# A fused attention and channel-mix kernel with its PSUM banks, its instruction order and its engine choices written anew

## The chip, the cores and the metric

The kernel runs on one core of one Trainium2 chip. The metric is the device time of one execution in microseconds (us). The time before is 250.7 us, the median of three runs (250.73, 250.70, 248.66).

A core has five engines that run their own instruction lists in order and wait for each other by semaphores: PE (matmuls; its weight loads are shown apart as PEld), DVE, ACT and POOL for work on tiles, and SP, which here only issues DMAs. PE writes PSUM alone, which has eight banks of 512 float32 columns; DVE and ACT read PSUM, POOL does not.

## The reference

Inputs are q, k, v of 4 batches, 8 heads, 768 positions, 64 channels, a projection of 64 x 6, and the weights of a channel mix. What is computed:

```python
q_bits = einsum(q, proj) > 0                    # 6 bits a row, the same for k
mask = q_bucket[..., None] == k_bucket[..., None, :]
scores = where(mask, q @ k.T / 8, -1e9)
attn = exp(scores - max); attn /= attn.sum(-1) + 1e-9
x = (attn @ v)                                  # heads side by side: B, 768, 512
xk = mu_k * x + (1 - mu_k) * x_prev             # x_prev: one position earlier
xr = mu_r * x + (1 - mu_r) * x_prev
kk = relu(xk @ w_k) ** 2                        # 512 -> 1024
out = sigmoid(xr @ w_r) * (kk @ w_v)            # 1024 -> 512
```

## The kernel before, in words

**Pairs.** The 32 heads are worked in 16 pairs of two heads (n = 0 to 15, four pairs a batch). For a pair the kernel loads q and k (lines 471 to 481) and v (486), scales q and k into a float16 upper part (`hi`, lines 556, or 554 on ACT) and subtracts it for a lower part (`lo`, 559), and lets a DMA transpose (`tr`, 563) put both into tile `a`, with channels on the partitions. Pairs 0 and 1 are prepared by head instead (`add_prep_first`: 616 to 621), transposed on PE (635) and copied out of PSUM (639).

**Bits.** `bits` (587) multiplies `a` with the projection, 24 matmuls in column groups. DVE turns the signs into numbers (`bx`, 591), and two or four small DMAs from SP (`row`, 599) put them as six extra rows into `a`, so that a score of rows whose bits differ falls far below the others and its exponential vanishes. For pair 0 the bits go straight into `a` (657, then 663 on ACT or 665 on DVE).

**Scores and values.** A pair has nine score steps of 1024 columns, two PSUM banks each: two to four matmuls (708), then one exponential on ACT (712) into `pt`. The value product (`oo`, 736 and 741) takes 36 matmuls of 65 columns in three slices; DVE divides by the row sum (`rc`, `ob`, 751 to 758). The result is transposed (DMA 768, or PE 794 and a copy 798), shifted by one position (`xs`, 776 and 778) and mixed (829 to 841) into `xk` and `xr`. The sums over v that a row without a partner needs (`vsum`, 509 to 515) and a bfloat16 copy of v (`va`, 501) run on POOL or DVE.

**MLP.** After four pairs a batch's MLP can start: `kp` (859, four matmuls of 384 columns, 64 such groups in all), ReLU on ACT (864) or DVE (866), a square on DVE (869), `r` (884) and its tanh (887), `v` (896), the product (903) and the store (907).

**What sets the order.** Each operation is put into a plan with `add(engine, duration, ...)`. `add_on` gives a choice of engines, taken from the table `WHERE` (line 40). The list `ORDER` (line 70) is the written sequence of all 1386 operations; each engine's instructions follow it. `schedule` (line 199 on) walks it and, with the durations of the plan, gives each score step the pair of banks among (0,1), (2,3), (4,5) and each other PSUM tile the bank among 7 to 3 that comes free first. The two mu vectors of 512 values are loaded by ACT's queue value by value (422) and lowered by one on DVE (424). Seven matmuls on zeros run at the start (390). The SP queue issues loads, transposes, rows and stores in one order.

The choice of engines for `hi` (line 568) is an example of `add_on`, with duration, whether it takes the SBUF access that DVE and POOL share in the plan, and the call:

```python
add_on({"DVE": (DVE_C(768 * m, 2), 1, lambda hi=hi: hi(nc.vector)), "ACT": (ACT_C(768 * m), 0, lambda hi=hi: hi(nc.scalar)),
        "POOL": (2.15 * m, 1, lambda hi=hi: hi(nc.gpsimd))}, R("hi", n), f"hi{n}", f"hi{n}{side}", r=rn, w=nh_h)
```

In the lists below an operation is named as in the code: `sc7_6` is score step 6 of pair 7, `hi4q` the upper part of q of pair 4, `kp0_1_1` half 1 of the second 128 columns of batch 0's first MLP product. Head 0 of a pair has j = 0, the second head j = 1.

Of the kernel before, what the change touches and what calls it, by code (L numbers as in the profile page):

```python
# [16 lines left out]

LAG = {"PE": 0.21, "ACT": 0.21, "DVE": 0.15, "POOL": 0.18, "SP": 1.8, "GQ": 2.0}
# [17 lines left out]
def R(kind, n):  # L36
# [99 lines left out]
class Plan:  # L136
# [42 lines left out]
    def sequence(self):  # L179
        if ORDER:  # L180
            return [self.ops[i] for i in ORDER]
# [17 lines left out]
    def schedule(self):  # L199
# [9 lines left out]
        for o in order:  # L209
            e = "POOL" if o.eng == "GQ" else o.eng  # L210
            if o.svc and o.eng != "GQ":
                queue.append(o)
# [752 lines left out]
```

## Time and profile before

| | |
|---|---|
| median of three runs | 250.7 us |
| the runs | 250.73, 250.70, 248.66 us |
| span of the profiled execution | 251.3 us |
| first exponential starts | 13.81 us |
| last matmul ends | 248.1 us |
| PE, DVE, ACT, POOL busy | 236.9, 195.4, 179.1, 27.9 us |
| instructions of PE, DVE, ACT, POOL | 2609, 471, 225, 73 |
| exponentials (line 712) | 144, mean 1.040 us, together 138.8 us |
| DMA | 44.56 MB, mean 177 GB/s |

A row of a timeline gives start, duration, engine, line, operation, tiles (out<-in) and shape, and in brackets the idle time of the engine before it and what ended it. `SPq` and `ACTq` are DMA issues of these queues. Rows of groups give count, busy time, mean duration in ns, idle time before and what ended most of it. Matmuls overlap, so one matmul's duration is longer than its share of PE's time; the time from start to start counts. Idle time of an engine that nobody waits for costs nothing.

### The profile page before, as it was taken

How to read it: one execution, taken by the hardware profiler on the slowest of the kernel's cores; microseconds unless marked ns; L12 is line 12 of the kernel's file. 1: busy time of each engine (PE TensorE's matmuls, PEld its weight loads, DVE VectorE, ACT ScalarE, POOL GpSimd, SP SyncE). 2: the span in 40 equal slices, each digit the busy share in tenths (PEclk: the TensorE clock that was granted, in tenths of full speed). 3: DMA queues.
4: the chain of work that ended last, by engine and by line, in shares of the span. 5: the costliest groups of instructions: out<-in, count | busy, mean ns of one | idle time of the engine just before them, and what ended most of it. 6: DMA issues, size and time to landing. Idle time of an engine off the chain costs nothing.

```text
span 251.3 us, 6510 instructions
## 1 busy us (share of the span) xinstructions
PE 236.9 (94%) x2609; PEld 147.6 (59%) x2609; DVE 195.4 (78%) x471; ACT 179.1 (71%) x225; POOL 27.9 (11%) x73
## 2 busy tenths in 40 slices
PE   6886799999799998999999999999999999999993
PEld 2444578876566655666467566655865654545442
DVE  3795679889788889898998999899787878376322
ACT  5596689999799978996878899988787223332220
POOL 5002240541302031100001100100000000000000
PEclk9799799999999999999999999999999999999998
DMA  6999999999989999999999996793231030022223
GB/s 187 308 178 251 220 215 191 267 249 189 213 292 241 204 293 292 273 201 269 184 333 186 184 185 158 210 230 57 90 64 44 0 128 28 13 83 86 83 85 125
DMA packets 75194, 44.56 MB, mean 177 GB/s; under 512 B 55524, under 2 KB 70172, under 8 KB 75164
## 3 DMA queue, kind: packets, MB, share of 16 engines
q1 hardware_dynamic: 74028, 44.15, 72.8%
q8 instruction: 20, 0.33, 0.6%
q10 hardware_dynamic: 1136, 0.01, 0.3%
q14 instruction: 10, 0.08, 0.1%
HBM read 24.12 MB, written 6.29 MB: 121 GB/s over the span
## 4 chain that ended last, share of the span: by engine, by line
PE 75%; DMA 11%; DVE 8%; SPq 3%; ACT 1%; issue 1%; DVEq 0%
PE ps_all L708 19%; PE ps_all L896 17%; PE ps_all L859 13%; PE ps_all L741 12%; PE ps_all L884 8%; DMA nat<-in_k_dram 5%; PE ps_all L587 4%; DMA nat<-in_q_dram 3%; DMA a<-bx 2%; DMA os<-in_moe_w_k_dram 1%; DVE nh L559 1%; DVE nh L556 1%; PE ps_all L736 1%; ACT pt L712 1%; PE ps_all L794 1%
## 5 line engine op out<-in xcount | busy, mean ns | idle before, releaser
L712 ACT ACTIVATE pt<-ps_all 128x1024 bf16<-128x1024 f32 x144 | 138.8, 1040 | 21.1 <-PE ps_all L708 19.8
L708 PE MATMUL ps_all<-a 128*128 128x512 f16 (+3 forms) x408 | 80.6, 318 | 5.1 <-DMA a<-bx 3.9
L708 PEld LDWEIGHTS <-a 128*128 128x128 f16 x408 | 35.3, 98 | 26.7 <-DMA a<-bx 4.7
L859 PE MATMUL ps_all<-xk,wk 128*128 128x384 bf16 x256 | 49.0, 326 | 0.9 <-DVE kr L866 0.9
L896 PE MATMUL ps_all<-wv,k 128*128 128x512 bf16 (+1 forms) x200 | 45.9, 370 | 0.6 <-DVE os L903 0.6
L741 PEld LDWEIGHTS <-pt 128*128 128x128 bf16 x1152 | 42.1, 98 | 6.9 <-issue 1.1
L741 PE MATMUL ps_all<-va,pt 128*128 128x65 bf16 x1152 | 43.9, 194 | 0.0
L859 PEld LDWEIGHTS <-wk 128*128 128x128 bf16 x256 | 24.5, 98 | 17.6 <-issue 1.6
L896 PEld LDWEIGHTS <-k 128*128 128x128 bf16 x200 | 19.4, 98 | 20.6 <-issue 0.7
L864 ACT ACTIVATE kr<-ps_all 128x384 bf16<-128x384 f32 x33 | 15.8, 493 | 19.2 <-DVE k L869 12.7
L887 ACT ACTIVATE rs<-ps_all 128x512 f32<-128x512 f32 x24 | 14.2, 603 | 20.9 <-PE ps_all L884 19.0
L559 DVE SCALAR_TENSOR_TENSOR nh<-nat,nh 128x768 f16<-128x768 f32 x28 | 27.3, 976 | 1.1 <-ACT nh L554 0.6
L903 DVE SCALAR_TENSOR_TENSOR os<-rs,ps_all 128x512 f32<-128x512 f32 (+1 forms) x25 | 16.5, 662 | 14.7 <-PE ps_all L896 9.9
L869 DVE TENSOR_TENSOR k<-kr 128x384 bf16<-128x384 bf16 x64 | 21.5, 350 | 3.7 <-ACT kr L864 3.5
L884 PE MATMUL ps_all<-wr,xr 128*128 128x512 bf16 x96 | 23.8, 379 | 0.0
L866 DVE TENSOR_SCALAR kr<-ps_all 128x384 bf16<-128x384 f32 x31 | 17.1, 555 | 8.3 <-PE ps_all L859 6.6
L758 DVE TENSOR_TENSOR ob<-ps_all,rc 128x384 bf16<-128x384 f32 (+1 forms) x36 | 18.3, 511 | 1.0
L884 PEld LDWEIGHTS <-xr 128*128 128x128 bf16 x96 | 9.0, 98 | 10.0 <-ACT kr L864 0.3
L587 PE MATMUL ps_all<-a,p0g 128*32 128x256 f16 (+1 forms) x180 | 13.4, 276 | 1.3 <-DMA a<-nh 1.3
L556 DVE TENSOR_SCALAR nh<-nat 128x768 f16<-128x768 f32 x22 | 12.3, 557 | 3.0 <-DMA nat<-in_q_dram 2.5
L587 PE MATMUL ps_all<-a,p1g 128*32 128x256 f16 (+1 forms) x180 | 12.9, 273 | 0.0
L841 DVE TENSOR_TENSOR xr<-tm,xt 128x768 bf16<-128x768 f16 (+1 forms) x18 | 9.4, 520 | 0.4
(94 smaller groups left out, 187.4 us busy)
## 6 DMA issues: line engine op xcount, KB each, us to landing
vn<-in_v_dram SPq DMA_DIRECT2D x16, 384.0 KB
out_dram<-os SPq DMA_DIRECT2D x23, 256.0 KB
nat<-in_k_dram SPq DMA_DIRECT2D x15, 384.0 KB
nat<-in_q_dram SPq DMA_DIRECT2D x15, 384.0 KB
wst<-in_moe_w_k_dram SPq DMA_DIRECT2D x2, 512.0 KB
wst<-in_moe_w_r_dram SPq DMA_DIRECT2D x2, 512.0 KB
wst<-in_moe_w_v_dram SPq DMA_DIRECT2D x2, 512.0 KB
a<-bx SPq DMA_DIRECT2D x48, 9.0 KB
```

Source lines behind the costliest of these rows:

```text
L559: nc.vector.scalar_tensor_tensor(out=nh[:, :, D:P], in0=nat.rearrange("p j (c d) -> p (j c) d", d=D), scalar=QS, in1=nh[:, :, 0:D], op0=AL ...
L587: nc.tensor.matmul(ps[g_ * wid : (g_ + 1) * wid, 0:FW], w_[:, m_ - 1 - x : m_ - 1 - x + wid], a_t[sa][:, i, x % NFOLD * FW : (x % NFOLD + ...
L708: nc.tensor.matmul(ps[:, lo - s * STEP : hi - s * STEP], side_a["k"][sa][:, j, jc * P : (jc + 1) * P], side_a["q"][sa][:, j, q0 : q0 + hi ...
L712: nc.scalar.activation(out=pt_t[sp][:, s * STEP : (s + 1) * STEP], in_=ps_t[plan.slot[nm]], func=AF.Exp, bias=EBIAS, scale=ESC)
L741: nc.tensor.matmul(oo[:, (ic - c0) * 65 : (ic - c0) * 65 + 65], pt_t[sp][:, o : o + P], va_t[sa][:, j, jc, 0 : D + 1], start=(not uc and i ...
L758: nc.vector.tensor_tensor(out=ob_t[so][:, c0:c1, j * D : (j + 1) * D], in0=oo[:, :, 0:D], in1=rc_t[sr][:, 1, c0:c1].unsqueeze(2).to_broadc ...
L859: nc.tensor.matmul(ps[:, 0:HALF], wk_sb[:, d, fc * P : (fc + 1) * P], xk_t[mx[d]][:, h * HALF : (h + 1) * HALF], start=(d == 0), stop=(d = ...
L866: nc.vector.tensor_scalar(out=kr_t[sk], in0=sm(nm)[:, 0:HALF], scalar1=0.5 ** 0.5, scalar2=0.0, op0=ALU.mult, op1=ALU.max)
L869: nc.vector.tensor_tensor(out=k2_t[s2][:, h * HALF : (h + 1) * HALF], in0=kr_t[sk], in1=kr_t[sk], op=ALU.mult)
L884: nc.tensor.matmul(sm(nr), xr_t[mx[d]][:, c * P : (c + 1) * P], wr_sb[:, d, :], start=(d == 0), stop=(d == NDC - 1))
L896: nc.tensor.matmul(sm(nv)[:, lo:hi], k2_t[(b * NFC + fc) % NK2][:, c * P : (c + 1) * P], wv_sb[:, fc, lo:hi], start=(fc == 0), stop=(fc == ...
L903: nc.vector.scalar_tensor_tensor(out=os_t[so][:, lo:hi], in0=rs_t[s1][:, lo:hi], scalar=1.0, in1=sm(nv)[:, lo:hi], op0=ALU.add, op1=ALU.mult)
```

## The change

The operations are the same but for the load of mu; what changes is which engine does which, in which order they are written, and which PSUM bank each gets.

- A table `SLOT` names the first bank of each of the PSUM tiles; `schedule` only reads it and checks that no bank is held twice. The durations are no longer used for that. Score steps stay on banks (0,1), (2,3), (4,5), the others on 7 to 3.
- `ORDER` is another sequence of 1387 operations. The first four loads are k and q of the second head, then k and q of the first (before: k of the second, q of the first, q of the second, k of the first). Loads of pair 1 come ahead of those of pair 2.
- `WHERE` moves work: `hi` is on POOL 15 times (before never), on DVE 18 times (27), on ACT 3 times (9); partial sums of v on POOL 34 times (18), weight casts on POOL 7 times (4), on ACT never (twice).
- mu is loaded as eight rows of 128 values, turned by one matmul with an 8 x 8 identity, and lowered by one by one DVE instruction that reads PSUM.
- The seven matmuls at the start remain. A second group of dummy matmuls can be switched on (`NWARM2`) and is at 0. Other switches that come with it (`STEPS`, `ROWD`, `ROW_ACT`) are at values that change nothing.
- The last two pieces of the last MLP product change places: the one in halves (`v3_5`) comes before `v3_4`.

PE's order from pair 15's bits to its first score: before `bits15 sc14_7 sc14_4 sc13_4 v1_3 v1_3 oo13_0 oo13_0 oo13_0 sc14_3 oo14_0 sc14_5 oo14_0 oo13_1 oo13_1 oo13_1 sc15_1`; after `bits15 oo13_1 sc14_0 oo13_0 sc14_1 sc14_4 oo13_0 oo13_0 kp1_4_0 kp1_6_0 sc15_2`.

DVE's order at the start: before `hi0k1 lo0k1 lo0q0 lo0q1 hi0k0 lo0k0 evt0q01 evt0q00 hi1k1 evt0k00 lo1k1 lo1k0 hi2 lo2 beb0q10`; after `hi0k1 lo0k1 hi0q1 lo0q1 evt0k10 lo0k0 hi0q0 lo0q0 hi1k0 lo1k0 beb0q10` (`beb0q10` is the bit row of line 665).

```diff
+BANKS = {"sc": 2, "s3": 3, "sm": 1}
...
-    "vsum2": "DVE", "vsum2b": "DVE", "vsum2c": "POOL", "hi3q": "DVE", "hi3k": "DVE", "xt2_0": "DVE", "xs2_0": "DVE", "xt2_3": "DVE",
+    "xs1_0": "POOL", "xj1": "POOL", "va2": "DVE", "vsum2": "DVE", "vsum2b": "POOL", "vsum2c": "POOL", "hi3q": "POOL", "hi3k": "DVE",
...
+SLOT = {
+    "warm": 7, "mu": 6, "t0q00": 7, "b0q00": 7, "t0q01": 5, "b0q01": 3, "t0k00": 7, "b0k00": 7, "t0k01": 6, "b0k01": 5, "t0q10": 5, "b0q10": 2,
...
     def schedule(self):
+        used, held = set(), {}
+        order = [self.ops[i] for i in ORDER]
         for o in order:
...
             if o.take is not None:
+                name, size = o.take[1], BANKS[o.take[0]]
+                self.slot[name] = SLOT[name]
+                held[name] = set(range(SLOT[name], SLOT[name] + size))
...
-                choices = [(i, (2 * i, 2 * i + 1)) for i in self.pairs] if cls == "sc" else [(b, (b,)) for b in self.banks]
-                choices = [(max(t, *(bank_free[b] for b in bs)), k, i, bs) for k, (i, bs) in enumerate(choices) if not any(used[b] for b in bs)]
-                t, _, self.slot[name], bs = min(choices)
...
-    for t, src, key in ((muk, moe_mu_k, "muk"), (mur, moe_mu_r, "mur")):
-        def f_mu(t=t, src=src):
-            with nc.allow_non_contiguous_dma(reason="512 values"):
-                nc.scalar.dma_start(out=t, in_=src.rearrange("(c p) -> p c", p=P))
...
+    for i_, src in enumerate((moe_mu_k, moe_mu_r)):
+        add("ACT", 0.42, -19.0, lambda i_=i_, src=src: nc.scalar.dma_start(out=mu8[i_ * NDC : (i_ + 1) * NDC, :], in_=src.rearrange("(c p) -> c p", p=P)),
+            w=[("mu8", i_)], at=0.75, svc=0.05, off=1.5, land=1.05, name=f"ldmu{i_}")
+    add("PE", 0.12, 1.0, lambda: nc.tensor.matmul(sm("mu")[:, 0 : 2 * NDC], mu8, id8, start=True, stop=True),
+        r=["id8", ("mu8", 0), ("mu8", 1)], w=[("mu",)], take=("sm", "mu", 0), name="mu")
```

More of the change, by code (lines that the diff above doesn't have):

```diff
@@ L195, in moved @@
-    @staticmethod
-    def moved(t, work):
-        return t + work * (1.25 if t < 9.3 else 1.0)
-    def schedule(self):
-        free = {e: 0.0 for e in ("PE", "ACT", "DVE", "POOL", "SP")}
-        bank_free = [0.0] * 8
-        used = [False] * 8
-        count = {"sc": 0, "sm": 0, "moe": 0}
-        held = {}
-        dma_free = tr_free = after = 0.0
-        port = [0.0, 0.0]
-        queue = []
-        order = self.sequence()
+    def schedule(self):
+        used, held = set(), {}
+        order = [self.ops[i] for i in ORDER]
@@ L209, in schedule @@
         for o in order:
-            e = "POOL" if o.eng == "GQ" else o.eng
-            if o.svc and o.eng != "GQ":
-                queue.append(o)
-            t = max([free[e], o.at] + [queue[-9].vis if o.svc and o.eng != "GQ" and len(queue) > 8 else 0.0] + [self.ops[d].own if self.ops[d].eng == o.eng and not self.ops[d].svc else self.ops[d].vis for d in o.deps])
             if o.take is not None:
-                cls, name, moe = o.take
-                if count[cls] >= self.most[cls] or (moe and count["moe"] >= self.moe_most):
+                name, size = o.take[1], BANKS[o.take[0]]
@@ L221, in schedule @@
-                held[name] = (cls, bs, moe)
-                for b in bs:
-                    used[b] = True
-                count[cls] += 1
-                count["moe"] += moe
-            o.start = t
-            dur = o.dur
-            if o.port:
-                dur += max(0.0, port[e == "DVE"] - t)
-                port[e != "DVE"] = t + dur
-            if e == "SP":
-                dur += after
-                after = 0.3 * o.tr
-            if o.tr:
-                dma_free += 0.5 * (dma_free > t)
-                dur = max(dur, dma_free - 1.0 - t, tr_free + 0.1 - t)
@@ L237, in schedule @@
-            o.took = dur
-            free[e] = t + dur
-            lag = o.lag
-            if o.svc:
-                first = max(t + o.off, dma_free)
-                dma_free = self.moved(first, o.svc)
-                lag = max(0.9, dma_free + o.land - t - dur)
-                if o.tr:
-                    tr_free = dma_free
-            o.own = t + dur + 0.1 * (e in ("DVE", "ACT"))
-            o.vis = t + dur + lag
-            for name in o.give:
-                cls, bs, moe = held.pop(name)
-                for b in bs:
-                    used[b] = False
-                    bank_free[b] = o.vis
-                count[cls] -= 1
-                count["moe"] -= moe
@@ L255, in schedule @@
-        self.end = max(o.start + o.took for o in order)
+                used |= held[name]
+            for name in o.give:
+                used -= held.pop(name)
         return order
@@ L298 @@
     ROW_ACT = ()
+    ROWD = ()
     DIRECT = (0,)
@@ L324 @@
     bx_t = [buf([P, S // NFOLD], FP16, f"bx{i}") for i in range(NBX)]
+    if ROWD:
+        bdp = ctx.enter_context(tc.tile_pool(name="bd", bufs=1, space=bass.MemoryType.DRAM))
+        bd_t = [bdp.tile([P, FW], FP16, name=f"bd{i}", tag=f"bd{i}") for i in range(NBX)]
     vn_t = [buf([P, 2, HALF], FP32, f"vn{i}") for i in range(NV)]
@@ L361 @@
         px_t[g_] = [buf([P, P // g_ + 4 * NFOLD // g_], FP16, f"p{i}g{g_}") for i in range(2)]
-    muk = buf([P, NDC], FP32, "muk")
-    mur = buf([P, NDC], FP32, "mur")
-    ps_t = [ps_all[:, i * STEP : (i + 1) * STEP] for i in range(4)]
+    mu8 = tm_t[1].bitcast(FP32)[0 : 2 * NDC, 0:P]
+    id8 = buf([2 * NDC, 2 * NDC], FP32, "id8")
+    mu_t = buf([P, 2 * NDC], FP32, "mu")
+    muk, mur = mu_t[:, 0:NDC], mu_t[:, NDC : 2 * NDC]
     plan = Plan((0, 1, 2), (7, 6, 5, 4, 3), {"sc": 3, "sm": 5}, 3)
@@ L389 @@
     for i in range(NWARM):
-        add("PE", 0.43, -20.0 + 0.1 * i, lambda: nc.tensor.matmul(sm("warm"), wz[:, 0:P], wz, start=True, stop=True),
-            r=["wz"], w=["warm"], take=("sm", "warm", 0) if i == 0 else None, give=["warm"] if i == NWARM - 1 else [])
+        add("PE", 0.2155, -20.0 + 0.1 * i, lambda: nc.tensor.matmul(sm("warm"), wz[:, 0:P], wz, start=True, stop=True),
+            r=["wz"], w=["warm"], take=("sm", "warm", 0) if i == 0 else None, give=["warm"] if i == NWARM - 1 else [], name="warm")
+    for i in range(NWARM2):
+        add("PE", 0.2155, -7.5 + 0.15 * i, lambda: nc.tensor.matmul(sm("warm2"), wz[:, 0:P], wz, start=True, stop=True),
+            r=["wz"], w=["warm2"], take=("sm", "warm2", 0) if i == 0 else None, give=["warm2"] if i == NWARM2 - 1 else [], name="keep")
     add("ACT", 1.5, -9.5, lambda: nc.scalar.activation(out=tb[:, 0:1], in_=tb[:, 1:2], func=AF.Exp), r=["tb"], w=["tb0"], at=0.75, name="table")
@@ L696, in add_scores @@
     def add_scores(n):
-        sa, sp = n % NAQ, n % NPT
-        for s in range(NSTEP):
+        sa, sp, w = n % NAQ, n % NPT, STEP(n)
+        for s in range(NSTEP(n)):
             nm = f"sc{n}_{s}"
@@ L705, in f @@
             def f(nm=nm, s=s, ps_=ps_):
-                ps = ps_t[plan.slot[nm]]
+                ps = ps_all[:, plan.slot[nm] * 512 : plan.slot[nm] * 512 + w]
                 for lo, hi, j, jc, q0 in ps_:
-                    nc.tensor.matmul(ps[:, lo - s * STEP : hi - s * STEP], side_a["k"][sa][:, j, jc * P : (jc + 1) * P],
+                    nc.tensor.matmul(ps[:, lo - s * w : hi - s * w], side_a["k"][sa][:, j, jc * P : (jc + 1) * P],
                                      side_a["q"][sa][:, j, q0 : q0 + hi - lo], start=True, stop=True)
             def g(nm=nm, s=s):
-                nc.scalar.activation(out=pt_t[sp][:, s * STEP : (s + 1) * STEP], in_=ps_t[plan.slot[nm]],
+                nc.scalar.activation(out=pt_t[sp][:, s * w : (s + 1) * w], in_=ps_all[:, plan.slot[nm] * 512 : plan.slot[nm] * 512 + w],
                                      func=AF.Exp, bias=EBIAS, scale=ESC)
-            T = n + s / NSTEP + X("sc", n)
+            T = n + s / NSTEP(n) + X("sc", n)
             add("PE", sum(MM(p_[1] - p_[0]) for p_ in ps_), T, f,
                 r=need + [("a", side, sa, j) for side in "qk" for j in heads],
-                w=[(nm,)], take=("sc", nm, 0), name=nm)
-            add("ACT", ACT_C(STEP), T, g, r=[(nm,), "tb0"], w=[("pt", sp, s)], give=[nm], name=f"exp{n}_{s}")
+                w=[(nm,)], take=("sc" if w == 1024 else "s3", nm, 0), name=nm)
+            add("ACT", ACT_C(w), T, g, r=[(nm,), "tb0"], w=[("pt", sp, x) for x in range(s * w // 512, (s + 1) * w // 512)], give=[nm], name=f"exp{n}_{s}")
     def add_pv(n):
```

59 lines of the change are left out of this document (29 added, 30 removed), and 195 rows, old and new, of tables (ORDER, SLOT, WHERE).

## The prediction

> **What bounds the kernel now.** I read the page's engine table, then the span in stages, then the waits of PE and ACT, then the instructions around the waits. Columns of the stages: length, busy time and instructions of PE, PEld, DVE, ACT, POOL, then granted clock, DMA share, GB/s.
>
> ```profile
> PE 236.9 (94%) x2609; PEld 147.6 (59%) x2609; DVE 195.4 (78%) x471; ACT 179.1 (71%) x225; POOL 27.9 (11%) x73
> ...
> PE 75%; DMA 11%; DVE 8%; SPq 3%; ACT 1%; issue 1%; DVEq 0%
> ```
> ```profile
> 13.80:27.30 13.50, 9.08 (x94) 5.59 (x93) 10.04 (x19) 9.20 (x11) 1.67 (x2) 1.00 0.97 238
> 27.30:94.80 67.50, 65.79 (x942) 46.39 (x941) 55.87 (x137) 62.53 (x72) 16.49 (x32) 0.97 1.05 233
> 94.80:194.40 99.60, 98.69 (x1207) 62.71 (x1207) 88.28 (x223) 83.77 (x101) 5.99 (x14) 1.00 0.80 185
> 194.40:248.00 53.60, 53.03 (x316) 28.00 (x314) 32.42 (x77) 16.02 (x32) 0.00 (x0) 1.00 0.18 70
> ```
> ```profile
> 13.80:94.80 81.00, 68.08 (x72) 0.98 1.04 234
> ```
>
> The waits quoted further on are those of 27.3 to 94.8. The cuts are the first exponential (13.8), the first of pair 1 (27.3), the end of the 72nd of 144 (94.8) and of the last (194.4). From 94.8 on PE is filled: MLP matmuls lie between the scores. Before that ACT paces: 62.5 of 67.5 us busy, with the exponentials (third fence, line 712 alone) at 68.08/72 = 0.946 us each. So an idle microsecond of ACT counts ahead of 94.8, one of PE behind it, and MLP work that PE no longer does early is paid late.
>
> **Start and pair 1.** The single largest wait is that for the bit rows of pair 1.
>
> ```profile
> 9.12 0.36 DVE L618 TENSOR_SCALAR nh<-nat 128x384 f16<-128x384 f32 x1 [1.51 <-DMA nat<-in_k_dram]
> ...
> 9.66 1.02 DVE L621 SCALAR_TENSOR_TENSOR nh<-nat,nh 128x384 f16<-128x384 f32 x2
> 10.59 0.56 DVE L556 TENSOR_SCALAR nh<-nat 128x768 f16<-128x768 f32 x1
> 11.18 0.96 DVE L559 SCALAR_TENSOR_TENSOR nh<-nat,nh 128x768 f16<-128x768 f32 x1
> 12.17 0.95 DVE L665 TENSOR_SCALAR a<-ps_all 6x768 uint16<-6x768 uint16 x1
> ...
> 13.18 1.03 PE L708 MATMUL ps_all<-a 128*128 128x512 f16 x6 [0.99 <-DVE a L665]
> ...
> 13.81 2.86 ACT L712 ACTIVATE pt<-ps_all 128x1024 bf16<-128x1024 f32 x3 [0.60 <-PE ps_all L708]
> ...
> 19.61 0.28 PE L587 MATMUL ps_all<-a,p1g 128*64 128x256 f16 x2
> ...
> 20.00 0.42 DVE L591 TENSOR_SCALAR bx<-ps_all 128x256 uint16<-128x256 uint16 x1
> ...
> 20.45 2.36 SPq L599 DMA_DIRECT2D a<-bx  x2
> 20.47 0.37 ACTq L422 DMA_DIRECT2D muk<-in_moe_mu_k_dram  x1
> ...
> 26.63 1.70 PE L708 MATMUL ps_all<-a 128*128 128x512 f16 x7 [3.91 <-DMA a<-bx]
> ```
>
> The first score waits for line 665, and DVE does pair 2's line 556 and 559 (10.59 to 12.14) ahead of it. In the new order DVE goes hi1k0, lo1k0, then this bit row. The first of these still needs the fifth load, at 9.12 behind the same bytes: 9.12 + 0.36 + 0.55 + 0.95 and gaps makes 11.1, plus score and hand-over (13.81 - 13.18) 11.8; ACT's own list ahead of it, one more load conversion, makes it 12.0. So the first exponential comes 1.8 us earlier (0 to 2).
>
> It does not all last. The new ACT order puts one 768-column conversion, two bit conversions and two evictions among the nine exponentials of pair 0: 9 x 0.946 + 3.5 ends at 24.0, where it was 23.3. DVE's list up to bits1 (lo1q1, lo1k1, hi2, an eviction, a bit row, lo2, lo1q0, lo2, a bit row, two evictions) ends at about 17.9, so its matmuls end near 19.7, as now (19.61 + 0.28). From there to the first score pair 1 took 26.63 - 19.89 = 6.7 us. The lower bound is 4.1: bx and hand-over 0.56, two rows 1.53, landing at most 2.05 by the case of pair 5 below. With 4.1 nothing waits behind 24.0; with 6.7 the score comes at 26.4. Two loads stand ahead of the rows either way, but the 512 single values of mu (ACT queue, 20.47) are gone: I take the middle, 25.4, the exponential at 26.0 instead of 27.27. **Term 1: -1.3** (-2.9 to +0.5). The mu matmul, its 8-column eviction and the small identity cost 0.1 us of PE: nothing.
>
> **From pair 1 to the 72nd exponential.** ACT now does 63 x 0.946 = 59.6 us of exponentials and 3 us of ReLUs and a cast; new are two ReLUs instead of seven and no cast: 59.6 + 2 x 0.49 = 60.6.
>
> ```profile
> L864 ACT ACTIVATE kr<-ps_all 128x384 bf16<-128x384 f32 x33 | 15.8, 493 | 19.2 <-DVE k L869 12.7 <-PE ps_all L859 3.2 <-DVE kr L866 2.2
> ```
> ```profile
> ACT pt L712 <- PE ps_all L708: 6.8, 4, 3.9
> ACT kr L864 <- DVE k L869: 1.8, 1, 1.8
> ```
>
> The idle time in this stage is 67.5 - 62.5 = 5.0 (the two rows are its waits; the 3.9 lies ahead of 27.3). It was made by late scores and by ReLUs behind a blocked DVE; the new order has both kinds, so I keep 5.0, bounds 0 and 9. 65.6 instead of 67.5: **Term 2: -1.9** (-6.9 to +2.1).
>
> In exchange less MLP work lies in this part. Ahead of the 72nd score stand 32 matmuls of line 859 instead of 51, and 468 PV matmuls instead of 504.
>
> ```profile
> 103.59 1.09 PE ps_all L741 x36
> ...
> 213.65 4.55 PE ps_all L859 x28
> ```
>
> 19 x 0.1625 + 36 x 0.030 = 4.2 us come later, where PE has no gap to hide them. **Term 3: +4.2** (no other value unless PE finds gaps behind 94.8).
>
> **Rows behind it.** PE work written between the end of a pair's bits and its first score, with these durations (score 0.43): pairs 7, 9, 11, 14, 15 have 5.0, 4.6, 4.6, 4.5, 4.1 us, pairs 5 and 13 some 5.9. For pair 15: four PV slices of 12 (1.5), three scores (1.3), two line-859 groups of four (1.3). In the old order the shortest lead after pair 2 is 6.1.
>
> ```profile
> 58.77 1.53 SPq L599 DMA_DIRECT2D a<-bx  x2
> ...
> 61.91 1.03 PE L708 MATMUL ps_all<-a 128*128 128x512 f16 x4
> ...
> 84.99 0.28 PE L587 MATMUL ps_all<-a,p1g 128*32 128x256 f16 x4
> 85.06 1.38 SPq L447 DMA_DIRECT2D k<-in_moe_w_v_dram  x1
> ...
> 85.70 0.41 DVE L591 TENSOR_SCALAR bx<-ps_all 128x256 uint16<-128x256 uint16 x1
> ...
> 87.06 3.13 SPq L599 DMA_DIRECT2D a<-bx  x4
> ...
> 94.18 0.61 PE L708 MATMUL ps_all<-a 128*128 128x256 f16 x3
> ```
>
> Pair 5's third score (the third of the matmuls from 61.91, at 62.35) ran 2.05 us after its last row was issued without waiting; pair 8 took 94.18 - 85.27 = 8.9 from its bits, held by a weight load on SP and a loaded DMA, and its weight load waited 0.6. So a lead needs 4.1 to 6.7 (8.9 at worst). I take 5.0, nearer the fast end, since only two rows are needed and pairs 14 and 15 meet few loads: 0.4 + 0.4 + 0.5 + 0.9 at pairs 9, 11, 14, 15, less the 0.6: **Term 4: +1.6** (-0.6 at 4.1; at 6.7 it is 2.1 + 2.1 + 2.2 + 2.6 + 0.8 - 0.6 = +9.2). Pair 7 lies in term 2.
>
> **Casts moved to POOL.** 15 hi conversions, 16 partial sums of V, 3 weight casts leave DVE and ACT. DVE has slack, so alone this gains nothing; it costs where both want SBUF.
>
> ```profile
> 27.62 0.99 POOL L501 CAST va<-vn 128x768 bf16<-128x768 f32 x1 [2.28 <-DMA vn<-in_v_dram]
> ...
> 27.97 1.46 DVE L559 SCALAR_TENSOR_TENSOR nh<-nat,nh 128x768 f16<-128x768 f32 x1
> ```
> ```profile
> L559 DVE SCALAR_TENSOR_TENSOR nh<-nat,nh 128x768 f16<-128x768 f32 x28 | 27.3, 976 | 1.1 <-ACT nh L554 0.6
> ...
> L501 POOL CAST va<-vn 128x768 bf16<-128x768 f32 x6 | 5.6, 930 | 25.6 <-DMA vn<-in_v_dram 19.3 <-PE ps_all L741 6.1 <-PE ps_all L859 0.2
> ```
>
> Here line 559 took 1.46 beside the cast instead of 0.98: it waited the cast out. No row has a hi conversion on POOL; bounds are 0.93 (the cast of the same shape) and the 2.15 that the old file's plan carries at line 569. Its price for that cast, 0.85 at line 504, lies near the row, so I take 2.15. Between the 9th and the 72nd exponential stand eight: DVE's work on SBUF is by estimate 36 us (13 lo at 0.98, 23 us of hi, mixing, squares and sums), POOL's 19.4 + 8 x 2.15 = 36.6, together 72.5 (62.7 at 0.93), with 65.6 us of stage. The means contain such waits already, so the true sum is lower: I add nothing to term 2, and keep it as a rival. The Trainium skill ("GPSIMD Engine Reference", section Engine selection) calls one-input work on GpSimd roughly line-rate, which is the 0.93 end; by it the sum stays the same and the rival below loses most of its chance.
>
> **The end.** The last piece becomes a 512-column one.
>
> ```profile
> 245.67 0.69 DVE L903 SCALAR_TENSOR_TENSOR os<-rs,ps_all 128x512 f32<-128x512 f32 x1 [0.41 <-PE ps_all L896]
> ...
> 247.07 1.03 PE L896 MATMUL ps_all<-wv,k 128*128 128x256 bf16 x8 [0.57 <-DVE os L903]
> ...
> 248.14 0.42 DVE L903 SCALAR_TENSOR_TENSOR os<-rs,ps_all 128x256 f32<-128x256 f32 x1 [1.12 <-PE ps_all L896]
> ```
>
> The eviction grows by 0.27 and the wait of 0.57 goes: **Term 5: -0.3.** Banks written in the source cost nothing themselves: same matmuls, same tiles. There were no dummy matmuls in the middle before, so their absence changes nothing. The 7 at the start stay.
>
> **Sum:** 251.3 - 1.3 - 1.9 + 4.2 + 1.6 - 0.3 = 253.6. The profiled span is 0.6 above the median 250.7 of the three runs, so **253.0**. Its own range, terms 2 and 4 varied by half their bounds, is 249.5 to 257.
>
> **Rivals.** (1) Faster: rows land in 4.1 us everywhere, so terms 1 and 4 go to their ends and ACT idles 2 us instead of 5 before the 72nd exponential: 253.0 - 1.6 - 3.0 - 2.2 = 246.2. For it: pair 5; against it: pairs 1 and 8. It falls below 248.2 once the leads suffice and ACT's idle time is under 3. (2) The shared access of DVE and POOL becomes the bound of that stage: 72.5 us instead of 65.6 there, 253.0 + 6.9 = 260. For it: the 1.46; against it: half of DVE's work (ob, rc, ReLU, line 591) reads PSUM. The Trainium skill ("SBUF — State Buffer", Who interferes with whom) states an exclusive lock for the whole instruction, which the 1.46 bears out. (3) Rows take 6.7 us: 253.0 + 7.6 = 260.6. (4) The orders do not matter, since PE's total is the same and gaps only move: 250.7.
>
> **Chances.** Forecast 0.50, rival 1 0.24, rival 2 0.08, rival 3 0.08, rival 4 0.10. About 1% is what a measurement of this kernel can tell from no change: 248.2 to 253.2. Faster: 0.22 of rival 1. Same: rival 4, 0.02 of rival 1, 0.24 of the forecast, together 0.36. Slower: 0.26 of the forecast and rivals 2 and 3, 0.42. The range leaves out the outer tenths: 246.5 to 260.
>
> **What the profile would show.** First exponential at 12.0; pair 1's wait on a<-bx 1 to 2 us; the 72nd exponential ending near 91.6; waits of PE on a<-bx at pairs 7, 9, 11, 14, 15; POOL near 75 us busy, line 559 above 0.98; behind the last exponential some 69 us of MLP and PV instead of 53.6 (20 matmuls of line 859 more, 40 of 0.216 us of lines 884 and 896, 108 of PV). I am wrong if no wait on a<-bx is left (rival 1), or if DVE's waits on POOL lead the list (rival 2).

## The result and the profile after

The changed kernel takes 259.4 us (median of four runs, 258.9 to 260.02), the kernel before 249.84 (four runs, 248.66 to 250.73): a ratio of 1.0452 [1.0389, 1.0515], slower. That ratio is the one of the fast runs; the two medians alone give 1.038. The forecast was 253.0, range 246.5 to 260, with 0.42 on slower.

The page of after: the engine table, the chain of waits by engine, and two groups.

```profile
PE 236.4 (92%) x2592; PEld 146.8 (57%) x2611; DVE 190.9 (74%) x439; ACT 174.5 (68%) x219; POOL 84.7 (33%) x112
...
PE 52%; DVE 20%; DMA 12%; issue 5%; POOL 5%; ACT 2%; SPq 1%; DVEq 0%; POOLq 0%; ACTq 0%
...
L537 POOL TENSOR_SCALAR nh<-nat 128x768 f16<-128x768 f32 x13 | 30.7, 2363 | 24.0 <-DMA nat<-in_q_dram 11.8
...
L540 DVE SCALAR_TENSOR_TENSOR nh<-nat,nh 128x768 f16<-128x768 f32 x28 | 29.9, 1073 | 0.9 <-POOL nh L537 0.6
```

PE's work is the same to 0.5 us and DVE has less of it than before (195.4). But DVE now holds 20% of the chain that ends last, where it held 8% in the profile of the forecast (1% in a second one of before); PE holds 52% instead of 75% (90% in the second).

The execution behind the forecast's profile was longer than a usual one. In every later run of the kernel before, the time is 1.8 to 2.0 us above the span, so its span of 251.3 means about 253.2, against medians of 248.4 to 249.8 in the comparisons here. A second profile of the kernel before (`b2_before` below: span 247.4, time 249.31) is therefore the better neighbour of after (257.5, 259.31). Its chain of waits:

```profile
PE 90%; DMA 5%; DVE 1%; ACT 1%; issue 1%; SPq 1%; DVEq 0%
```

Both by stages, cut at the first exponential, the 18th (end of pair 1), the 72nd, the last one, and the last matmul; first before, then after:

```profile
0.00:13.80 13.80, 11.15 (x58) 5.17 (x59) 9.26 (x21) 7.48 (x12) 3.88 (x25) 0.88 0.85 240
13.80:35.70 21.90, 18.61 (x221) 12.55 (x219) 15.74 (x29) 17.66 (x20) 5.29 (x9) 0.92 1.08 239
35.70:90.70 55.00, 53.79 (x807) 38.73 (x805) 48.88 (x124) 53.49 (x62) 12.51 (x26) 1.00 0.99 245
90.70:190.50 99.80, 99.27 (x1203) 63.27 (x1212) 88.18 (x223) 83.78 (x101) 6.10 (x14) 1.00 0.80 186
190.50:244.20 53.70, 52.87 (x312) 28.02 (x314) 32.44 (x77) 16.02 (x32) 0.00 (x0) 1.00 0.18 70
244.20:247.40 3.20, 0.02 (x1) 0.00 (x0) 0.42 (x1) 0.00 (x0) 0.00 (x0) 0.96 0.19 67
```
```profile
0.00:11.50 11.50, 8.84 (x49) 4.31 (x50) 6.77 (x14) 5.36 (x10) 5.50 (x21) 1.00 0.82 246
11.50:33.30 21.80, 18.27 (x213) 11.98 (x212) 16.72 (x31) 20.39 (x24) 12.54 (x20) 1.00 0.92 225
33.30:90.10 56.80, 52.08 (x777) 36.94 (x778) 46.00 (x102) 52.08 (x58) 35.95 (x39) 1.00 1.01 241
90.10:183.60 93.50, 89.30 (x1086) 56.56 (x1096) 76.12 (x185) 76.97 (x91) 30.37 (x33) 1.00 0.81 194
183.60:253.70 70.10, 67.90 (x476) 37.06 (x482) 44.58 (x110) 19.72 (x40) 0.30 (x1) 1.00 0.18 63
253.70:257.50 3.80, 0.00 (x0) 0.00 (x0) 0.69 (x1) 0.00 (x0) 0.00 (x0) 0.91 0.38 138
```

In each row the first number behind the cut is the stage's length and the second PE's busy time; their difference is PE's idle time. Stage by stage it was 2.7, 3.3, 1.2, 0.5, 0.8, 3.2 us, together 11.7, and is 2.7, 3.5, 4.7, 4.2, 2.2, 3.8, together 21.1. PE's busy time differs by 0.7. So 9.4 of the 10.1 us are idle time of PE: 3.5 between pair 1 and the 72nd exponential, 3.7 from there to the last one, 2.0 behind it.

One stage of one profile is only good to about 2 us. The stage from the end of pair 1 to the 72nd exponential took 56.8 us in after, and 56.6, 54.7 and 54.8 us in three kernels below whose lists are the same up to there (`n3_tail`, `e6_waits2`, `e8_banks4`). From the end of pair 1 to the last exponential these four agree better: 150.2, 150.5, 149.8 and 151.2 us. Of the 3.5 us, 2.0 are left against e6 and e8.

PE's waits in after from 90 us on show no single cause:

```profile
PE ps_all L889 <- DVE os L896: 1.0, 1, 1.0
PE ps_all L701 <- DMA a<-bx: 1.0, 2, 0.8
PE ps_all L568 <- DMA a<-nh: 0.9, 1, 0.9
PE ps_all L889 <- DVE wv L432: 0.9, 1, 0.9
PE ps_all L852 <- DVE ob L751: 0.7, 1, 0.7
PE ps_all L509 <- DVE os L896: 0.5, 1, 0.5
PE ps_all L852 <- DVE kr L859: 0.4, 1, 0.4
```

Five of the seven end with a DVE instruction. In four of these (the rows of 889 on `os`, 852 on `ob`, 509 on `os` and 852 on `kr`) the matmul does not read what DVE wrote; it waits for the PSUM bank that this DVE instruction has just emptied. The waits for bit rows, which the forecast feared, make 1.0.

### The profile page after: what moved, and what is told of

Same layout as the page of the kernel before. It is cut to its first block, busy times and chain, and to the rows that moved or that the text cites. A ratio compares the mean times of both kernels' runs of the same rounds, so it can differ in the third digit from the quotient of the medians.

```text
span 257.5 us, 6534 instructions
## 1 busy us (share of the span) xinstructions
PE 236.4 (92%) x2592; PEld 146.8 (57%) x2611; DVE 190.9 (74%) x439; ACT 174.5 (68%) x219; POOL 84.7 (33%) x112
## 3 DMA queue, kind: packets, MB, share of 16 engines
q1 hardware_dynamic: 74028, 44.15, 67.9%
## 4 chain that ended last, share of the span: by engine, by line
PE 52%; DVE 20%; DMA 12%; issue 5%; POOL 5%; ACT 2%; SPq 1%; DVEq 0%; POOLq 0%; ACTq 0%
PE ps_all L889 13%; PE ps_all L701 11%; PE ps_all L852 11%; PE ps_all L877 7%; PE ps_all L734 5%; PE ps_all L568 4%; DVE nh L540 4%; DMA vn<-in_v_dram 4%; DMA nat<-in_q_dram 3%; POOL nh L537 2%; DMA a<-nh 2%; DMA out_dram<-os 2%; DVE ob L751 2%; DMA a<-bx 2%; DVE os L896 2%
## 5 line engine op out<-in xcount | busy, mean ns | idle before, releaser
L701 PE MATMUL ps_all<-a 128*128 128x256 f16 (+3 forms) x408 | 80.0, 316 | 5.1 <-DMA a<-bx 3.1
L852 PE MATMUL ps_all<-xk,wk 128*128 128x384 bf16 x256 | 48.6, 326 | 2.1 <-DVE xk L834 0.9
L701 PEld LDWEIGHTS <-a 128*128 128x128 f16 x408 | 34.3, 97 | 26.3 <-issue 8.0
L734 PEld LDWEIGHTS <-pt 128*128 128x128 bf16 x1152 | 43.2, 97 | 9.9 <-issue 1.6
L889 PE MATMUL ps_all<-wv,k 128*128 128x512 bf16 (+1 forms) x191 | 44.9, 370 | 2.3 <-DVE os L896 1.0
L734 PE MATMUL ps_all<-va,pt 128*128 128x65 bf16 x1152 | 45.4, 193 | 0.0
L537 POOL TENSOR_SCALAR nh<-nat 128x768 f16<-128x768 f32 x13 | 30.7, 2363 | 24.0 <-DMA nat<-in_q_dram 11.8
L852 PEld LDWEIGHTS <-wk 128*128 128x128 bf16 x256 | 24.5, 98 | 19.6 <-issue 3.5
L889 PEld LDWEIGHTS <-k 128*128 128x128 bf16 x200 | 19.0, 98 | 21.4 <-issue 2.3
L540 DVE SCALAR_TENSOR_TENSOR nh<-nat,nh 128x768 f16<-128x768 f32 x28 | 29.9, 1073 | 0.9 <-POOL nh L537 0.6
L862 DVE TENSOR_TENSOR k<-kr 128x384 bf16<-128x384 bf16 x64 | 23.2, 382 | 5.8 <-ACT kr L857 5.4
L572 DVE TENSOR_SCALAR bx<-ps_all 128x256 uint16<-128x256 uint16 x15 | 6.3, 421 | 11.0 <-PE ps_all L568 9.5
L490 POOL TENSOR_TENSOR vt<-vn 128x384 f32<-128x384 f32 x7 | 8.0, 1143 | 19.4 <-DMA vn<-in_v_dram 12.2
```

The lines of the kernel that those rows point to most:

```text
L537: e.tensor_scalar(out=o, in0=x, scalar1=QS, scalar2=None, op0=ALU.mult)
L540: nc.vector.scalar_tensor_tensor(out=nh[:, :, D:P], in0=nat.rearrange("p j (c d) -> p (j c) d", d=D), scalar=QS, in1=nh[:, :, 0:D], op0=AL ...
L701: nc.tensor.matmul(ps[:, lo - s * w : hi - s * w], side_a["k"][sa][:, j, jc * P : (jc + 1) * P], side_a["q"][sa][:, j, q0 : q0 + hi - lo], ...
L734: nc.tensor.matmul(oo[:, (ic - c0) * 65 : (ic - c0) * 65 + 65], pt_t[sp][:, o : o + P], va_t[sa][:, j, jc, 0 : D + 1], start=(not uc and i ...
L852: nc.tensor.matmul(ps[:, 0:HALF], wk_sb[:, d, fc * P : (fc + 1) * P], xk_t[mx[d]][:, h * HALF : (h + 1) * HALF], start=(d == 0), stop=(d = ...
L862: nc.vector.tensor_tensor(out=k2_t[s2][:, h * HALF : (h + 1) * HALF], in0=kr_t[sk], in1=kr_t[sk], op=ALU.mult)
```

## The experiments

Theory A: POOL's casts make DVE late. Theory B: the written PE order runs too close behind what it needs. Theory C: the written banks lose the time. Most kernels here are tables put together anew; the diffs show a line of each.

### Single tables exchanged

`e1_mu`: before, with mu loaded as in the diff above.

```diff
-                nc.scalar.dma_start(out=t, in_=src.rearrange("(c p) -> p c", p=P))
...
+    add("PE", 0.12, 1.0, lambda: nc.tensor.matmul(sm("mu")[:, 0 : 2 * NDC], mu8, id8, start=True, stop=True),
```

> The kernel before, with only the load of mu changed: eight rows of 128 values, one matmul with an identity, one DVE instruction; engines, order and the bank rule are those of before. Theory M (the 512 single values of mu on ACT's queue hold back pair 1's bit rows): the wait of PE on a<-bx at pair 1 falls from 3.9 us to 2 or less and the time from 249.8 to about 248. Rival (that wait has another cause, the two loads ahead of the rows): wait and time stay, 249.8 within 0.7.

248.96 us, ratio 0.9979 [0.9938, 1.0021]: no difference that can be told. In its profile PE waited 2.3 us for pair 1's rows (3.9 and 3.0 in the two profiles of before). But of two later profiles with this start at a granted clock of 1.00, the one with mu by rows (`h2_second_after`) and the one with mu value by value (`n2_before_nohi`) both show 2.4 us. So theory M is not borne out.

`e2_engines`, `e3_order`: the engine tables exchanged.

```diff
 e2, on the order of before
-    "hi4q": "DVE",
+    "hi4q": "POOL",
...
 e3, on the order and banks of after
-    "hi4q": "POOL",
+    "hi4q": "DVE",
```

> The order of before (with mu by rows, as in e1_mu) and its bank rule, but every engine choice of the kernel after: 15 hi on POOL, 34 partial sums on POOL. Theory A (the casts on POOL make DVE late, through the shared access and because lo waits for hi): most of the loss appears here, 255 to 259. Theory B (the written sequence loses the time: MLP deferred behind the last score, PE steps close behind what they need) and theory C (the banks lose it): the time of e1_mu within 1.5, so 248 to 251.

> The kernel after with its written sequence and its written banks, but every engine choice of the kernel before. Theory A (engines): the loss goes, 250 to 252. Theories B and C (sequence, banks): it stays, 257 to 260; the waits of PE behind the 72nd exponential remain some 5 us more than in the kernel before.

272.27 us (1.0899 [1.0839, 1.0959]) and 285.74 us (1.1481 [1.1377, 1.1585]). Neither theory expected this: each order with the other's engines is far worse than either kernel. Order and engines were written for each other, so exchanging a whole table tells nothing about where after loses.

`e4_banks`: other banks for 204 tiles of after.

```diff
-"kp0_7_0": 7,
+"kp0_7_0": 3,
```

> The kernel after with its sequence and engines, but with another bank for 204 of its 340 PSUM tiles: each gets the one that has been free longest in the written sequence, where that leaves a bank for the tiles behind it. Theory C (the written banks make PE wait for a bank that DVE has just been given to empty; in the kernel after such waits add up to 5.9 us, against 2.2 before): 254 to 256. Theories A and B (DVE is late, or PE's sequence is too close, whichever bank is named): 258.5 to 260.

271.17 us, 1.0861 [1.0806, 1.0916]. Theory C falls, the other way round: the written banks are 12 us better than this other choice. PE's waits in e4:

```profile
PE ps_all L701 <- ACT pt L705: 9.5, 19, 1.5
```

In after this wait is 0.7, once. In e4, 31 tiles that are not scores sit in bank 3 (12 in after) and 33 in bank 4 (27). They leave the scores fewer pairs of banks, and a score then waits for an exponential to empty its pair.

`e5_hi`: after with its 15 hi back on DVE (13) and ACT (2; the text below says 14 and 1).

```diff
-    "hi5q": "POOL",
+    "hi5q": "DVE",
```

> The kernel after, with only its 15 hi conversions on POOL put back on the engine they had before (14 on DVE, 1 on ACT). Theory A (the conversions on POOL, 2.36 us each, make lo, the transposes and so DVE's whole list late): 253 to 256; line 540 (lo) back near 0.98 us. Rival (the sequence was written for POOL doing them, DVE's list in that order has no room for 14 more): 259 to 263.

274.88 us, 1.1139 [1.103, 1.1248]: as the rival says, and more than it says. In this order DVE has no room for them; late weight casts alone hold PE 6.3 us (`L889 <- DVE wv L432`, 0.9 in after).

### Halves joined

The operations left over keep the second kernel's order, and each operation the engine and, but for 1 to 4 tiles, the bank of the kernel that it comes from:

```diff
-ORDER = second
+ORDER = first[:cut] + [i for i in second if i not in first[:cut]]
```

> Sequence, engines and banks of the kernel after up to the 18th exponential (the end of pair 1), and those of the kernel before for every operation that is left, mu by rows. Theory S (the written start of after is good and stands alone): the first exponential at 11.5, the 18th ends near 33.5 instead of 35.6 (e1_mu) or 37.1 (before), and the time is 2 to 3.5 below that of e1_mu: 245.5 to 247. Theory T (a start is worth only what the sequence behind it can use; PE work is what ends last): 248 to 250.

> Sequence, engines and banks of the kernel before up to the 72nd exponential (mu by rows), and those of the kernel after for every operation that is left. Theory U (after loses its time behind the 72nd exponential, where PE is the bound and its waits came to some 6 us against 1.5): the 72nd exponential ends near 92.5 as in e1_mu, and 163 us follow it: 256 to 258. Theory V (after loses it ahead, by MLP work not done under the scores): 249 to 251.

> The counterpart of h2: the kernel after up to the 72nd exponential, the kernel before for what is left. Theory U: 72nd exponential near 90.1, and the second part of before with 4.2 us of deferred MLP and PV work more: 249 to 251. Theory V: 256 to 258.

h1: 254.72 us (1.0295 [1.0232, 1.0358]); h2: 255.95 (1.0334 [1.0279, 1.0389]); h3: 255.11 (1.0327 [1.0242, 1.0412]). Theories U and V both fail, since h2 and h3 both lose. h1 has its 18th exponential at 33.7 us, but then eight scores wait 3.6 us for an exponential: the seam itself costs, so h1 says nothing about the start. h3 loses right behind its seam: from the 72nd to the 90th exponential it takes 36.1 us (28.7 in `b2_before`), and behind the 90th 128.3 (128.0). From the 72nd exponential to the last PE is busy 104.0 us (99.3 in b2): the difference is work that after's first part left over. The rest, some 2.9 us more idle time of PE there, may be the seam. h2 is the cleaner one: its 72nd exponential ends at 89.3, after's at 90.1. The written first part is not faster than the old one at the same granted clock (1.00 in both). Behind the 72nd exponential h2 takes 164.3 us, b2 156.7.

### The reference again, and PE's waits covered

`b2_before`: no edit.

> The kernel before, unchanged, for a second profile. Theory P (the profiled execution that the forecast was made on was a slow one: clock 0.983, while the rows of its first 54 us show 0.88 to 0.94): at a clock of 0.99 or more the first exponential starts near 12.7, the 72nd ends near 90 instead of 94.8, the stage behind it stays at 156 to 157, and the span is 246 to 248. Rival (that profile was typical): the 72nd exponential again near 94, the span 250 to 252.

Span 247.4, 72nd exponential at 90.7, 156.7 us behind it: the forecast's profile was a long one, as theory P says. The clock is not shown as the reason: b2's was as low (0.88 up to the first exponential, which came at 13.80 again; 0.986 over the span), and the two profiles part most between the 36th and the 72nd exponential (41.0 and 38.5 us), where both had 1.00.

`e6_waits2` (PE's list, one of eight changes), `e7_waits12`, `e8_banks4`:

```diff
-bits9 sc8_6 kp0_4_0 kp0_4_0
+sc8_6 kp0_4_0 kp0_4_0 bits9
...
-"v1_4": 3
+"v1_4": 0
```

> The kernel after, with eight PE steps behind the 72nd exponential that wait 0.2 to 1.0 us each moved one to four steps later in PE's list (bits9, sc9_5, sc9_4, the second half of v0_0, mean10, kp1_0_0) or given a bank that is idle there (v1_4 bank 0, kp2_2_1 bank 1); every other list is untouched. Theory W (those waits are what the second part loses, and each has ready work right behind it): idle time of PE behind the 72nd exponential falls from 6.4 to 2 us and the time to 254 to 256. Rival X (DVE paces that part, a wait that is covered comes back a few steps later): 258 to 260.

> As e6_waits2, with three more waits ahead of the 72nd exponential covered (the rows of pairs 2 and 4, the second half of kp0_0_0 behind xk; together 3.1 us). If ACT paces that part, the 72nd exponential still ends at 89.5 to 90.1 and the time is that of e6_waits2 within 0.7; if PE's waits pace it, both come 2 to 3 us earlier.

> Only the four of these eight steps that waited for a bank being emptied (mean10, kp1_0_0, v1_4, kp2_2_1; 0.52 + 0.36 + 0.98 + 0.69 = 2.6 us). Theory W: 256.5 to 257.5. Rival X: 258.5 to 259.5.

259.73, 261.06 and 259.9 us (1.0469 [1.042, 1.0518], 1.0549 [1.0497, 1.06], 1.0509 [1.0445, 1.0573]). Theory W, a form of B, falls. In e6 the covered waits are gone, but from 90 us on PE waits for other work of the same engines (`L852 <- DVE os` 0.8, `L852 <- ACT rs` 0.7, `L734 <- DVE va` 0.7, `L852 <- DVE ob` 0.5). Its idle time from the 72nd exponential to the last matmul was 7.5 us in e6, 8.1 in e8 and 6.4 in after; theory W had 2. PE's waits are what is left over by something late.

### What is late

The chain of waits in after, a stretch without PE and one behind the last exponential (start, length, what):

```profile
130.42 0.55 DVE ob L751
130.96 0.47 DVE nh L537
...
131.77 0.55 DVE ob L751
132.32 0.47 DVE xk L834
132.79 0.47 DVE nh L537
133.26 0.34 DVE tm L830
...
133.62 1.27 DVE xk L834
...
135.90 0.69 DVE os L896
136.58 0.05 issue
136.63 0.23 PE ps_all L509
```
```profile
190.98 0.70 DVE os L896
191.70 0.33 SPq L900
192.03 0.05 issue
192.08 4.67 DMA out_dram<-os
...
196.84 0.69 DVE os L896
```

From 130.1 to 143.6 us the chain runs through DVE's instructions and the issue times between them; PE has 0.25 us of it. At 191 it is a store: there are three `os` buffers, and the fourth product waits for the first store.

`n3_tail`, `n1_after_nohi`, `n2_before_nohi`, `d1_before_dummy`, `n4_after_nolo`:

```diff
 n3
-            s1, so = (b * NSC + c) % NRS, (b * NSC + c) % NOS
+            s1, so = (b * NSC + c) % NRS, (b * NSC + c) % NOS if (b, c) < (1, 3) else NOS + (b * NSC + c) % 9
 n1
-"POOL": (2.15 * m, 1, lambda hi=hi: hi(nc.gpsimd))
+"POOL": (2.15 * m, 1, lambda hi=hi: None)
 n4
-            add("DVE", DVE_C(768 * m), R("lo", n), lo, r=rn + nh_h, w=nh_l, port=1, name=f"lo{n}")
+            add("DVE", DVE_C(768 * m), R("lo", n), lambda: None, r=rn + nh_h, w=nh_l, port=1, name=f"lo{n}")
 n2, inside hi
+                if nm in SKIP:
+                    return
 d1, behind each of the 13 hi
+                for j in range(4):
+                    nc.gpsimd.tensor_scalar(out=dmy, in0=side_nat[side][n % NQ][:, j // 2, (j % 2) * 192 : (j % 2) * 192 + 192].rearrange("p (c d) -> p c d", d=D), scalar1=QS, scalar2=None, op0=ALU.mult)
```

> The kernel after with the products from the fourth of batch 1 on written to nine more buffers (the tiles of q and k, idle by then) and with two tiles on banks 0 and 1, which nothing uses behind the last exponential. Theory C (behind the last exponential DVE waits 3.2 us once for a store of 4.7 us, and PE then twice for banks, 1.15 and 0.85 us): the stretch from the last exponential to the last matmul falls from 70.1 to about 68, the time to 256.5 to 257.5. Rival X (DVE and ACT have no room there, another wait follows): 258.5 to 260.

257.35 us, 2.05 below after (against before 1.0389 [1.0258, 1.0519]). Theory C of that text, the store buffers, holds: from the last exponential to the last matmul 67.9 us instead of 70.1, and PE has no idle time in it.

```profile
184.00:251.90 67.90, 67.89 (x484) 37.07 (x482) 44.69 (x110) 19.72 (x40) 0.29 (x1) 1.00 0.18 66
251.90:255.70 3.80, 0.00 (x0) 0.00 (x0) 0.69 (x1) 0.00 (x0) 0.00 (x0) 0.90 0.39 138
```

With the same two banks and without the buffers this stretch took 69.8 us (e6) and 69.4 (e8), so most of the 2.2 us are the buffers'.

> The kernel after with the 13 hi conversions of 768 columns that POOL does left out (lo then works on what the tile held before). Theory A (POOL's conversions make DVE late: lo waits for them and DVE's SBUF work beside them runs longer): DVE's extra time falls from 13.9 us to about 5, the chain of waits goes back to PE, and the time is 250 to 254. Rival B (the order of PE's and DVE's lists alone loses the time): 257 or more.

> The control: the kernel before with the same 13 conversions left out (11 on DVE, 2 on ACT). There they cost nothing that PE waits for, since PE paces: 247.5 to 249.6, within 0.5% of before. If it gains more than 2, leaving out work counts by itself, and n1 has to be read against that.

n1: 258.11 us (1.0395 [1.0314, 1.0476]); n2: 249.3 (1.001 [0.996, 1.0061]). Without the 13 conversions after is 1.3 us faster, so theory A in that form falls. DVE keeps its 20% of the chain. The control, before without them, does not change.

> The kernel before, with 13 conversions of 768 columns added on POOL (each in four instructions of 192 columns, read from the same loaded tile, written to a tile that nobody reads), at the place of the 13 hi that after moves. Nothing waits for them. Theory A by its shared-access half alone: DVE's extra time rises from 2.5 us by 5 to 9, and the time to 250.5 to 255. Rival (only lo's wait for a slow POOL matters, not the shared access): within 1 of before, 247.5 to 249.6.

254.52 us, 1.0249 [1.0159, 1.0339], within the range of theory A. But DVE's extra time (how it is counted stands at the end of the next section) rose only to 6.7 us, by some 4 instead of 5 to 9. The edit also took more than intended (49.4 us of POOL, four times 0.95 us a conversion), and POOL's dummies stand in the chain themselves (`POOL dmy L939 6%`): loading POOL costs the old order 5 us partly by making its partial sums late, not by the shared access alone.

> The kernel after with all 28 lo instructions of 768 columns left out (DVE is relieved of 29.9 of its 190.9 us, and the transposes wait for hi alone). Theory D (DVE's list is too full where PE waits for it): PE's idle time between the first exponential and the last matmul falls from 14.7 us to some 8, the time to 252 to 254. Rival E (the order of the hand-overs between PE, ACT, DVE and the DMA queue loses the time, not the amount of DVE's work): 256.5 or more.

253.26 us, 6.1 below after (1.0188 [1.0126, 1.025] against before): theory D. The chain and the stages from the first exponential on:

```profile
PE 69%; DMA 8%; DVE 8%; ACT 5%; issue 4%; SPq 3%; POOL 2%; DVEq 0%; ACTq 0%; POOLq 0%
```
```profile
10.70:31.80 21.10, 18.50 (x217) 12.26 (x217) 11.21 (x25) 20.22 (x24) 10.83 (x23) 1.00 0.99 241
31.80:86.30 54.50, 51.31 (x773) 36.88 (x770) 34.98 (x92) 51.31 (x58) 31.57 (x36) 1.00 1.00 251
86.30:177.40 91.10, 88.79 (x1085) 56.70 (x1095) 64.33 (x172) 76.84 (x92) 26.45 (x33) 1.00 0.84 199
177.40:247.40 70.00, 67.94 (x476) 37.07 (x482) 44.61 (x110) 19.72 (x40) 0.29 (x1) 1.00 0.18 64
```

DVE falls from 20% to 8% of the chain. The stage to the 72nd exponential shrinks from 56.8 to 54.5, the next from 93.5 to 91.1; the first of these alone proves nothing, since it took 54.7 in e6, but together, from the end of pair 1 to the last exponential, they take 145.6 us, where after, n1, n3, e6 and e8 took 149.8 to 151.2. The last stage stays at 70.0, as it must if the store buffers set it. PE's idle time in these four stages fell from 14.6 to 10.2 us, not to the 8 expected. Leaving lo out also lets the transposes start earlier. PE's own waits on transposes hardly change (0.9 us in after, 0.8 here), but what earlier transposes bring the other lists, the run does not tell. Before without lo was not tried; in b2 PE idles 2.6 us in all from the end of pair 1 to the last matmul, so there is less to win there.

`d2_defer`: five groups of batch 0 moved behind the 72nd score.

```diff
 PE's list
-kp0_2_0 kp0_2_0
...
 the score of the 72nd exponential
...
+kp0_2_0 kp0_2_0
```

> The kernel before (mu by rows, its banks written out) with five groups of four line-859 matmuls of batch 0, together 20 x 0.1625 = 3.25 us of PE, written behind the 72nd score instead of ahead of it, their ReLUs and squares with them. By term 3 of the forecast (ACT paces ahead of the 72nd exponential, so PE's relief there is worth nothing, and the work is paid later): 72nd exponential at most 1 us earlier, time 3 us above that of e1_mu and before, 251.5 to 253. Rival F (PE is as full ahead as behind, so the work only changes places): 72nd exponential 2 to 3 us earlier, time within 1 of 249.

261.51 us, 1.0506 [1.0444, 1.0568]: both miss. The 72nd exponential ended at 91.5 us (90.7 in b2, 92.5 in e1), so no gain ahead of it shows, which fits term 3 but is within what profiles of one kernel differ by. The next 18 exponentials took 43.5 us instead of 28.7: PE waited 3.6 us for a bank with a ReLU (`L579 <- DVE kr L870`) and for ACT. The price of deferring alone stays open.

## Why the prediction was wrong

The forecast adds 2.3 us to 250.7; the medians differ by 9.6, and the spans of b2 and after by 10.1. Against b2, by the forecast's parts: up to the 72nd exponential -3.2 forecast and -0.6 measured, from there to the last matmul +5.8 and +10.1, behind it -0.3 and +0.6. That 259.4 lies inside the range is luck: only rivals 2 and 3 reach that far, and neither came true as described. By its steps:

- **Term 1** (-1.3): at the far end of its bounds, and by luck. PE did not wait for the rows of pair 1:

```profile
20.17 1.78 SPq L592 DMA_DIRECT2D a<-bx  x2
...
23.72 0.60 PE L701 MATMUL ps_all<-a 128*128 128x256 f16 x3
...
24.35 1.02 ACT L705 ACTIVATE pt<-ps_all 128x1024 bf16<-128x1024 f32 x1 [0.31 <-PE ps_all L701]
```

  Pair 1's first exponential came at 24.35 (forecast 26.0, bound 24.4), directly behind the ninth, which ended at 24.04 (forecast 24.0). But the old order came there at 24.64 (h2) and 24.72 (n2) in the two profiles in which its granted clock stayed at 1.00, against 27.27 in the forecast's. So some 0.3 of the 2.9 us are the new order's, and mu has no visible part in them.
- **Term 2** (-1.9): 65.6 us forecast, 90.1 - 24.4 = 65.7 measured. But both terms were taken from a stage that was itself 4.1 us longer than in the second profile (72nd exponential at 94.8 against 90.7). Against b2 the first part gains 0.6 us, not 4.7, though less PE work lies in it (79.2 us busy against 83.6, a part of which is the lower clock at b2's start). PE's idle time there grew by 2.0 to 3.5, which the forecast did not ask about: it kept ACT's 5.0 and took that for the limit.
- **Term 3** (+4.2): the count is right, 1578 weight loads behind the 72nd exponential against 1521 before, 57 more (forecast 55). Its make-up is not: 13 more of line 859 (forecast 19), 34 of PV (36), and 8 of line 884, at 0.216 us each, that it left out. PE was busy 157.2 us there against 151.8, so 5.4 more instead of 4.2. That it is a cost because ACT paces ahead was not settled by d2.
- **Term 4** (+1.6) is the step that failed. It looked for PE's waits behind the 72nd exponential only where bit rows land. Pairs 7, 11, 14 and 15 had none; pair 9 waited 1.0 in two. The stages behind the 72nd exponential took 167.4 us where the forecast's terms make 162.0. Of these 5.4 us, 1.2 are the work that term 3 missed; the other 4.2 are idle time of PE (10.2 us, where the 4.7 of the forecast's profile and terms 4 and 5 make 6.0), mostly in hand-overs from DVE and, behind the last exponential, in waits that the stores caused. "DVE has slack" fits its busy share (78% before, 74% after), but in after DVE's list stood in the chain for 13 us on end, and leaving its lo instructions out won 6.1 (n4).
- **Term 5** (-0.3): the wrong sign. The wait of 0.57 went, but the end behind the last matmul is 3.8 instead of 3.2: 0.27 is the longer eviction, which the forecast had, and 0.3 lies behind it, where the last store now carries 512 columns instead of 256 (3.06 us from the end of the eviction to the end of the span, 2.77 before). And the products of batch 1, deferred behind the last exponential, came so densely that three store buffers did not do: 2.0 (n3).
- **The sum**: span and time are not the same thing. The execution's time was about 253.2, so 2.5 above the median and not 0.6. This slip cancels (253.6 + 1.9 - 2.5 is 253.0 again). What did harm is that stages of a long execution were subtracted; one more profile would have shown it. The forecast's own range is also added up wrongly: half of its bounds gives 249.4 to 258.8, not 249.5 to 257.
- **Rivals.** Rival 2 named the right time and the right engine, but the wrong place: the stage that it priced at 72.5 took 65.7, and the hi conversions themselves cost 1.3 (n1). POOL was busy 84.7 us (forecast 75), one conversion 2.36 (2.15). Rival 3 named the right time for the wrong reason. Rival 1's sign, that no wait on `a<-bx` is left, did not come either (3.1 us in four). Of "what the profile would show", the first exponential (11.48 for 12.0), the 72nd (90.1 for 91.6) and the 70.1 us behind the last one (69) came out; the row waits did not.

Shown: some 6 us go with the 28 lo instructions on DVE (n4) and 2 with the store buffers (n3); 0.6 is the end behind the last matmul. Only argued: why DVE is late with less work. Beside POOL its instructions run longer: each instruction set against the duration that a fifth of its kind and shape stay below, and the excesses over 0.06 us added up, they make 13.9 us in after and 2.3 in b2. Of the 13.9, 13.4 lie on 27 instructions that overlap one of POOL in time (161 of DVE's 439 do). Only 2.6 of it lie beside a hi conversion of 768 columns, most of the rest beside casts and partial sums. That fits n1: with those conversions gone 11.3 stay, and no run took POOL's other work away. In n4 it is 7.7, so n4 relieved DVE of both, work and extra time, and does not part them. Whether the shared access or DVE's order weighs more is open. No version beat the kernel before by more than can be told.

## What to carry to other kernels

Take a second profile of the reference before you subtract stages from it, and add what lies outside the span. Trust a sum of stages more than one stage: here one stage of unchanged code moved by 2 us from profile to profile. Where an order, a choice of engines and banks were written together, price a new one by PE's idle time stage by stage and by which engine holds the chain of waits, not by busy shares or by one kind of wait; a wait that is covered by hand comes back if another engine's list is what is late. When work is deferred to the end, count the buffers that its results leave by.

## What the runs showed of the hardware

- A conversion from float32 to float16 with a scale of 128x768 took POOL 2.36 us (in after) and one of 128x192 0.95 us (d1), where DVE took 0.56 in the forecast's profile. The Trainium skill ("GPSIMD Engine Reference", Engine selection) calls one-input work there roughly line-rate. The scaled conversion took 2.5 times POOL's plain cast of the same shape (0.93 in the forecast's profile), so that does not hold for both, and the measurement decides.
- The granted clock fell at the start of five of the seven profiles that begin with the old order and its engines, and in none that begin with the new order and its engines and banks nearly unchanged (after, e6 to e8, h1, h3, n1, n3, n4). The bit matmuls of the first 13.8 us, in b2 and in n2, where it did not fall:

```profile
L657 PE MATMUL ps_all<-a,p 128*32 128x384 f16 (+2 forms) x15 | 4.6, 472 | 0.0
```
```profile
L660 PE MATMUL ps_all<-a,p 128*32 128x384 f16 (+2 forms) x16 | 3.1, 328 | 0.0
```

  In the two profiles at 1.00 the first exponential came at 12.7 and 12.8 us (h2, n2), in the five with 0.88 at 13.8 to 14.2. So of the forecast's 1.8 us between the old and the new start, about 1 goes with the execution and not with the order. The order alone is not what keeps the clock up: with other banks (e4) or other engines (e5) the new one fell to 0.94 and 0.92 in its first 36 us.
